# Queries and keys through a bf16 copy in DRAM and DMA transposes, from the fourth batch on

## The chip, the cores and the metric

The kernel runs on one core of one Trainium2 chip. The metric is the time of one execution on the device in microseconds; the time before is the median of three runs. The engines are PE (TensorE, matmuls), DVE (VectorE), ACT (ScalarE), POOL (GpSimd) and SP (SyncE, which here only issues DMAs).

## The reference

Sparse attention over 8 batches of 8 heads, 576 positions of 64 numbers, followed by a bilinear feed-forward layer over the 4608 tokens. The first four heads of a batch attend to a local window, the other four to positions with the same residue modulo 32.

```python
scores = scale * np.matmul(q, k.transpose(0, 1, 3, 2))          # q, k, v: (8, 8, 576, 64)
rel = pos[:, None] - pos[None, :]
mask_local = (rel >= 0) & (rel < 32)
mask_strided = (rel >= 0) & (pos[None, :] % 32 == pos[:, None] % 32)
masks = [mask_local if h < 4 else mask_strided for h in range(8)]
attn = softmax(np.where(masks, scores, -1e9))
x = np.matmul(attn, v).transpose(0, 2, 1, 3).reshape(4608, 512)
out = ((x @ w_a) * (x @ w_b)) @ w_out                            # w_a, w_b: (512, 1536)
```

## The kernel before

**Tiles and slots.** The feed-forward layer is cut into nine tiles of 512 tokens (t = 0 to 8), and each tile into 16 slots: twelve `ffn_ab` (the two products of one block of 128 hidden columns, multiplied by DVE into `pf`) and four for the output product. Slot 16t+i is the i-th slot of tile t. A matmul result of `ffn_ab` sits in one of four PSUM banks (`mm` three, `tp` one): ACT copies the first product out (`a_sb`), DVE's `pf` multiply (line 648 or 650) frees the second. The output product of tiles 2 to 8 works with sums of blocks of `pf` (`ps`, made by DVE in `fast_s`, line 760), and tiles 7 and 8 do the same for the first products (`joint`), which needs sums of the weights `wa_sb` and `wb_sb`: `wsum_make` (line 666) makes eight of 128x1536, each in two instructions, the four of `wa_sb` on DVE and the four of `wb_sb` on POOL, in tile 6.

**Attention runs between the slots.** The attention of batch b is put into tile b-1; tile b is the first to need its result. It has eight units u: S (`S_p`, scores of two heads, line 389), exp on ACT, the mask on DVE (line 428), then V (`step_VT`, line 527, or `V_p`, line 467). `LATER` is the plan from batch 3 on, in slots of that tile: S0 at -1, V0 at 1, and so on to V5 at 11; `IN_Y` puts the rest into the output product. There is one `o` PSUM buffer, so the next V waits until DVE has taken the last one's result (lines 541 and 543 for batch 2 and the strided heads, after ACT's Ln and Exp at lines 536 and 537; line 493 for the local heads). Local results of batches 3 to 7 go to DRAM (`rows_out`, `xd`, step O) and come back transposed into `xT` (`rows_in`, step I, line 514, a DMA transpose on SP).

**How q and k come in, from batch 2 on.** POOL issues DMAs that cast to bf16, a head at a time: `load_qk`, line 213 for local heads into `kl` and `ql`, line 204 for strided heads into `natk` and `natq`. DVE transposes blocks of 32x32 (`step_D`, lines 328 and 333) into `tk` and `tq`. SP then moves them with DMAs from SBUF to SBUF (lines 343 and 347) into `kT` and, with zeros between, into `qz` (the zeros let one matmul with 128 rows serve two heads). `kT` and `qz` have two buffers, for odd and even batches. In the code, g0 = 16(b-2) is the first slot of tile b-2, in which batch b is brought in.

**Order.** Nothing is reordered: every engine, SP and POOL included, works through its own instructions in the order in which the program gives them. `do(i, ...)` puts a step behind slot i. From slot 14 on, POOL's part of a slot waits for that slot's `pf` or `y_sb` (a copy into `pace`, line 1060), so that its DMAs go out slot by slot. SP has no such pace: it goes on until a semaphore holds it.

Of the kernel before, what the change touches and what calls it, by code (L numbers as in the profile page):

```python
# [8 lines left out]
BF16 = mybir.dt.bfloat16  # L9
I16 = mybir.dt.int16  # L10
ALU = mybir.AluOpType
# [3 lines left out]
FIRST_D = 2  # L15
RL = 6
RS = 8
# [14 lines left out]
def kernel(  # L32
# [228 lines left out]

    held = {}
    paired = {}

# [54 lines left out]
    def step_D(b, z, nm, part):  # L321
        src = nats[b, nm, z == 1]
        if part == 0:
            tl[b, z, nm] = blocks(nm, z)
        t = tl[b, z, nm]
        if z == 0:
            i = slice(NY // 2 * part, NY // 2 * (part + 1))
            nc.vector.transpose(t.rearrange("p h (i y) -> p i h y", i=NY)[:, i],
                                src[:, i].rearrange("p i (h d) -> p i h d", h=2))
            last = part == 1  # L330
        else:

            nc.vector.transpose(
                t.rearrange("p h (r c) -> p r h c", r=RS)[:, :, :, YS * part:YS * part + 32],
                src[:, part].rearrange("p (r h d) -> p r h d", r=RS, h=2))
            last = part == 2
        if last:
            for nm, c in {"k": (("k", 0),), "q": (("q", 0), ("k", 1), ("q", 1))}[nm]:
                t = tl[b, z, nm]
                for e in range(2):  # L340
                    if nm == "k":
                        dst = kT_buf[b % 2][z][64 * e:64 * e + 64, c]
                        nc.sync.dma_start(out=dst[:, PAD:] if z == 0 else dst[:, :RS * GP], in_=t[64 * c:64 * c + 64, e])
                        continue
                    for j in range(2):
                        r0 = 64 * c + 32 * j
                        nc.sync.dma_start(out=qz_buf[b % 2][j][z][64 * e + 32 * j:64 * e + 32 * j + 32, c],
                                          in_=t[r0:r0 + 32, e])
                if (nm, c, z) == ("q", 0, 0) and b - 1 > FIRST_D:
                    rows_in(b - 1, 1)  # L350

    def rezero(b):

        for j in range(2):
            for t in qz_buf[b % 2][j]:
                nc.gpsimd.memset(t[32:64] if j == 0 else t[64:96], 0.0)

    def step_Tk(b, c):
        T_p(b, c, "k")
# [19 lines left out]
    def S_p(b, u):  # L379
# [4 lines left out]
        held[b, "st", u] = st  # L384
        if b > 0:
            sv = st.rearrange("p a (i n) -> p (a i) n", n=256)
            for i in range(G):
                k0 = (G * half + i) * (LW if c < 2 else GP)
                nc.tensor.matmul(sv[:, i, :2 * n].rearrange("p (j n) -> p j n", j=2), lhsT=kT[:, c % 2, k0:k0 + 128],  # L389
                                 rhs=qz_pair[b % 2][c // 2][:, :, c % 2, k0:k0 + n], start=True, stop=True)  # L390
            return
# [124 lines left out]
    def step_VT(b, u):  # L516
# [4 lines left out]
        for i in range(G):  # L521
            for j in range(2):
                if c < 2:
                    vt = vl_buf[b % 2][:, (2 * c + j) * 6 + 3 * half + i]
                else:
                    vt = vs_buf[b % 2][:, 2 * (c - 2) + j, 4 * half + i]
                nc.tensor.matmul(o[:, j, i * n:(i + 1) * n], lhsT=vt, rhs=p_cols(b, p, j, i, n, n)[:M], start=True, stop=True)  # L527

        r = sb.tile([128, RS * 4 * D], BF16, tag="xr", name="xr", bufs=2)[:64, :4 * W].bitcast(F32)
        r = r.rearrange("p (j w) -> p j w", j=2)  # L530
        if c < 2:
            sums = o[64:, :, :W]
# [33 lines left out]
    def step_X(b, c):  # L566
# [20 lines left out]
    LATER = {-1: "S0", 0: "S1", 1: "V0", 2: "S2", 3: "V1 O0", 4: "S3", 5: "V2", 6: "S4 I0", 7: "V3 O1", 8: "S5", 9: "V4",  # L587
             10: "S6",
             11: "V5"}
    IN_Y = {2: "S7", 6: "V6", 11: "V7"}  # L590
# [36 lines left out]
    def ffn_ab(t, f, mid, ab=None):  # L627
# [28 lines left out]
    wsum = [[h.rearrange("p (c g m) -> p c g m", c=2, g=FG) for h in homes] for homes in (  # L656
        [flat(vl_buf[0])[:, WS * z:WS * (z + 1)] for z in range(2)] + [flat(t)[:, :WS] for t in qz_pair[0]],
        [flat(vs_all[0])[:, WS * z:WS * (z + 1)] for z in range(2)] + [flat(nat_s[nm]) for nm in "qk"])]
    xsum = {t: flat(qz_pair[1][t - 7])[:, :8 * HT].rearrange("p (n c m) -> p n c m", n=4, c=2) for t in JOINT}

    def wsum_make(s, n, eng):
        w, s_ = (lambda e, j: wviews[s][:, j, :, :, e]), wsum[s]
        a, b, op = ((w(1, 0), w(1, 1), ALU.add), (s_[0], w(0, 0), ALU.subtract), (w(0, 0), w(1, 0), ALU.subtract),
                    (w(0, 1), s_[1], ALU.subtract))[n]
        for c in range(2):
            eng.tensor_tensor(s_[n][:, c], a[:, c], b[:, c], op=op)

    def x_part(t, j, k):
        x0 = TTOK * t % (XR * S) + HT * k
# [30 lines left out]
    def joint(t):  # L700
# [3 lines left out]
        for half, (plain, *gs) in enumerate(JOINT[t]):  # L704
            banks = {x: eight(x) for x in "Ya Yb Xb Zb Xa Za".split()}
            order = JOINT_ORDER[half].split()
            for at_, (k, m) in enumerate(order):
# [10 lines left out]
                else:  # L718
# [4 lines left out]
                    bank = banks[bank + m]  # L723
                    for s in range(2):
                        for c in range(2):
                            w = wsum[s][lhs][:, c, g] if isinstance(lhs, int) else wviews[s][:, lhs[1], c, g, lhs[0]]
# [182 lines left out]
    with tc.manual_schedule(engines={ENG.PE, ENG.SP, ENG.Pool, ENG.DVE, ENG.Activation}):  # L909
# [77 lines left out]
        for b in range(1, B):  # L987
            for pos, names in (STEPS.get(b) or {16 * (b - 1) + x: n for x, n in LATER.items()}).items():
                steps.setdefault(pos, []).append((b, names.split()))
            if b not in STEPS:  # L990
                for n, names in IN_Y.items():
                    steps["y", b - 1, n] = [(b, names.split())]
        steps[16 * (B - 2) + 9][-1][1].append("I1")

        at = {}

# [12 lines left out]
        for b in range(FIRST_D, B):  # L1009
            g0 = 16 * (b - 2)  # L1010
            if b == FIRST_D:
# [82 lines left out]
```

## Time and profile before

| | |
|---|---|
| Runs | 330.39, 330.40, 331.71 us, median 330.4 |
| Profiled execution | 331.63 us, span 329.9 us |
| TensorE clock | 1.0 throughout |
| Busy, share of the span | PE 96%, DVE 81%, PEld 64%, ACT 57%, POOL 55% |
| DMA queue of POOL | 85968 packets, 19.48 MB, 64.7% of 16 engines' span |
| DMA queue of SP | 25772 packets, 20.71 MB, 26.0% |
| Tile 1 from | 58 us (slot 16) |
| Tiles 2, 3, 4, 5, 6 from | 94, 128, 161, 195, 229 us |

The span is the profiled stretch; the execution's own time has 1.7 us around it. A line of a timeline reads: start, duration, engine, line, operation, output<-input, shape, count, and in brackets how long the engine was idle before it and who released it. A line of the waits reads: who waited for whom, total, number of waits, longest.

### The profile page before, as it was taken

To read this page: it belongs to the slowest core of one execution; us is meant where nothing else is said; L and a number is where in the kernel's file an instruction comes from. 1 tells how busy PE (TensorE), PEld (TensorE's weight loads), DVE (VectorE), ACT (ScalarE), POOL (GpSimd) and SP (SyncE) were. 2 spreads that over 40 slices of the span, in tenths; PEclk is the share of its full clock that TensorE was granted. 3 is DMA by queue.
4 is the path that set the end of the run, shared out by engine and by line. 5 is a ranking of instruction groups with operands and counts; after the bars stand their busy time and mean duration, and the time that the engine had idled before them with its cause. 6 is when DMAs were issued, how large, how long until landed. Compare 5 with 4: busy or idle time off the path is not lost.

```text
span 329.9 us, 7496 instructions
## 1 busy us (share of the span) xinstructions
PE 317.1 (96%) x2691; PEld 212.8 (64%) x2720; DVE 267.3 (81%) x551; ACT 188.7 (57%) x320; POOL 180.2 (55%) x295
## 2 busy tenths in 40 slices
PE   8999999999999999999999999999986799999995
PEld 6754555445555586557999875578543577787775
DVE  7766887888778889889889888988999977864882
ACT  6764764468764575457644764476544555525532
POOL 8845836899857444754475347632278405312350
PEclk9999999999999999999999999999999999999999
DMA  9999999899999999999999999998164013003003
GB/s 158 149 204 201 203 182 168 185 182 130 141 211 130 135 100 92 124 208 121 119 120 215 123 114 107 188 171 103 31 173 59 0 24 108 0 0 129 2 1 127
DMA packets 111920, 40.73 MB, mean 123 GB/s; under 512 B 89868, under 2 KB 108940, under 8 KB 111884
## 3 DMA queue, kind: packets, MB, share of 16 engines
q0 software_dynamic: 85968, 19.48, 64.7%
q1 hardware_dynamic: 25772, 20.71, 26.0%
q8 instruction: 21, 0.34, 0.4%
q14 instruction: 15, 0.12, 0.1%
q10 hardware_dynamic: 144, 0.07, 0.1%
HBM read 39.51 MB, written 11.06 MB: 153 GB/s over the span
## 4 chain that ended last, share of the span: by engine, by line
PE 72%; DMA 8%; DVE 8%; POOL 7%; issue 3%; ACT 1%; POOLq 0%; DVEq 0%
PE mm L624 32%; PE mm L818 13%; PE mm L880 5%; DMA vl<-in_v_dram 4%; DMA shared<-in_q_dram 4%; PE st L389 3%; PE o L527 2%; PE eA L624 2%; PE eXb L728 2%; PE eXa L728 2%; PE eB L624 2%; DVE ps L760 2%; POOL shared L198 2%; PE eYa L818 2%; DVE pf L648 2%
## 5 line engine op out<-in xcount | busy, mean ns | idle before, releaser
L624 PE MATMUL mm<-xT,wb_sb 128*128 128x512 bf16 (+1 forms) x373 | 85.0, 352 | 4.2 <-DVE pf L648 3.9
L624 PE MATMUL mm<-xT,wa_sb 128*128 128x512 bf16 (+1 forms) x360 | 83.9, 351 | 0.7
L645 ACT COPY a_sb<-mm 128x512 f32<-128x512 f32 x82 | 47.9, 585 | 49.0 <-PE mm L624 41.5
L624 PEld LDWEIGHTS <-wb_sb 128*128 128x128 bf16 x416 | 40.1, 98 | 39.9 <-issue 5.2
L624 PEld LDWEIGHTS <-wa_sb 128*128 128x128 bf16 x416 | 37.3, 98 | 22.7 <-DVE xT L543 0.3
L1060 POOL CAST pace<-pf 1x1 f32<-1x1 bf16 x71 | 22.8, 321 | 45.2 <-DVE pf L648 31.8
L648 DVE TENSOR_TENSOR pf<-a_sb,mm 128x512 bf16<-128x512 f32 x60 | 40.7, 679 | 6.4 <-PE mm L624 6.1
L410 ACT ACTIVATE p<-st 72x576 bf16<-72x576 f32 (+1 forms) x56 | 36.4, 650 | 16.2 <-PE st L389 16.0
L543 DVE TENSOR_TENSOR xT<-o,xr 64x288 bf16<-64x288 f32 x48 | 21.4, 445 | 13.5 <-ACT xr L537 13.0
L818 PEld LDWEIGHTS <-ps 128*128 128x128 bf16 x288 | 27.9, 98 | 3.9 <-DVE ps L760 0.7
L732 POOL TENSOR_TENSOR pf<-vl 128x256 bf16<-128x256 f32 x12 | 8.7, 729 | 30.8 <-DVE vl L741 30.8
L536 ACT ACTIVATE xr<-o 64x576 f32<-64x576 f32 x28 | 18.1, 647 | 12.6 <-PE o L527 12.3
L880 PE MATMUL mm<-wo_sb,pf 128*128 128x512 bf16 x93 | 23.2, 379 | 0.2
L818 PEld LDWEIGHTS <-pf 128*128 128x128 bf16 x216 | 20.1, 98 | 3.7 <-DVE pf L648 1.2
L244 POOL DMA_DIRECT2D vs<-in_v_dram x24 | 19.6, 818 | 5.0 <-PE mm L818 2.4
L760 DVE TENSOR_TENSOR ps<-pf 128x512 bf16<-128x512 bf16 (+2 forms) x42 | 21.6, 514 | 0.6
L818 PE MATMUL mm<-wf,ps 128*128 128x256 bf16 x180 | 21.5, 273 | 0.5 <-DVE ps L760 0.5
L537 ACT ACTIVATE xr<-xr 64x576 f32<-64x576 f32 x28 | 19.1, 683 | 0.9
L213 POOL DMA_DIRECT2D ql<-in_q_dram x24 | 15.9, 664 | 6.2 <-DMA wo_sb<-in_moe_w_out_dram 4.6
L213 POOL DMA_DIRECT2D kl<-in_k_dram x24 | 16.1, 671 | 5.3 <-issue 3.2
L791 ACT COPY y_sb<-mm 128x512 f32<-128x512 f32 x20 | 11.7, 585 | 12.1 <-PE mm L818 10.5
L650 DVE TENSOR_TENSOR pf<-a_sb,mm 128x512 bf16<-128x512 f32 x22 | 14.9, 677 | 4.5 <-ACT a_sb L645 2.7
(242 smaller groups left out, 640.0 us busy)
## 6 DMA issues: line engine op xcount, KB each, us to landing
out_dram<-y_sb SPq DMA_DIRECT2D x12, 512.0 KB, 5.5
out_dram<-y_sb SPq DMA_DIRECT2D x11, 256.0 KB, 4.2
vl<-in_v_dram POOLq DMA_DIRECT2D x6, 384.0 KB, 7.7
kl<-in_k_dram POOLq DMA_DIRECT2D x24, 72.0 KB, 3.1
ql<-in_q_dram POOLq DMA_DIRECT2D x24, 72.0 KB, 3.3
vs<-in_v_dram POOLq DMA_DIRECT2D x24, 72.0 KB, 4.2
wo_sb<-in_moe_w_out_dram POOLq DMA_DIRECT2D x4, 384.0 KB, 9.8
natk<-in_k_dram POOLq DMA_DIRECT2D x20, 72.0 KB, 3.5
```

Source lines behind the costliest of these rows:

```text
L213: nc.gpsimd.dma_start(out=t[32 * h:32 * h + 32], in_=src[b, h].rearrange("(i y) d -> y i d", y=32))
L244: nc.gpsimd.dma_start(out=vs_buf[b % 2][:, h, :, 0:D], in_=v[b, HL + h].rearrange("(p r) d -> p r d", r=RS))
L410: nc.scalar.activation(p_flat(p)[:M, :2 * W].rearrange("p (i n) -> p i n", n=2 * n), st[:M].rearrange("p a (i n) -> p (a i) n", n=256)[:, ...
L537: nc.scalar.activation(r, r, ACT.Exp, scale=-1.0)
L543: nc.vector.tensor_mul(dst.rearrange("d (p r) -> d p r", r=RS)[:, :, G * half:G * (half + 1)], o[:64, j, :W].rearrange("d (g p) -> d p g", ...
L624: nc.tensor.matmul(ps_[:, c0:c0 + n], lhsT=w[:, kk, 128 * f:128 * (f + 1)], rhs=xT[:, kk, x0:x0 + n], start=(kk == first and c0 == 0), sto ...
L645: nc.scalar.copy(a_sb, ab[0])
L648: nc.vector.tensor_mul(pf[:, f, :].rearrange("p (i a s) -> p a i s", i=2, s=16), halves(a_sb), halves(ab[1]))
L760: nc.vector.tensor_tensor(s[:, n], a, b, op=op)
L818: nc.tensor.matmul(bank[b][:, q], lhsT=lhs(g, q), rhs=rhs(g), start=k in "172" and q == 0 and g == 0, stop=g == FG - 1, skip_group_check=True)
L880: nc.tensor.matmul(ybank[j], lhsT=pf[:, f, 128 * j:128 * (j + 1)], rhs=wo_sb[:, f], start=(f == 0), stop=(f == FD - 1))
L1060: nc.gpsimd.tensor_copy(pace, done)
```

## The change

For batches 3 to 7, q and k go another way. POOL casts the local and the strided heads of k and of q into DRAM, four DMAs per batch in place of sixteen (`rows_load`, slots g0+1 to g0+4). SP brings each in by one DMA transpose (`rows_take`, slots g0+4, 6, 8, 10), keys straight into `kT`, queries into `tq`. DVE copies the queries' halves into the padded `qz` (`rows_pad`, slots g0+8, 9 for the local heads, g0+12, 13 for the strided ones). DVE's block transposes and SP's 24 transfers from SBUF to SBUF remain for batch 2 only.

With it: the strided heads are in another order, so `S_p` and `step_VT` take one head a unit, in as many matmuls of the same sizes, and `step_VT` writes 64x576 in one multiply. `rezero` clears other halves of the other `qz` buffer and moves from slot 14 to slot 33. `rows_in(b, 1)` moves to slot 9 of its tile for all batches. All sixteen weight-sum instructions are DVE's, eight in tiles 4 and 5 and eight in tile 6, at other places in SBUF.

```diff
+    def rows_load(b, nm, z):
+        t = rows[nm, z] = dram.tile([(S, NR)[z], (4, 8)[z] * D], BF16, tag=f"z{nm}{z}", name=f"z{nm}{z}", bufs=1)
+        h0 = b * H + HL * z
+        src = {"k": k, "q": q}[nm].rearrange("b h s d -> (b h) s d")[h0:h0 + HL]
+        if z:
+            nc.gpsimd.dma_start(out=t.rearrange("(h p) m -> h p m", h=HL), in_=src.rearrange("h (p r) d -> h p (r d)", r=RS))
+        else:
+            nc.gpsimd.dma_start(out=t.rearrange("s (h d) -> s h d", d=D), in_=src.rearrange("h s d -> s h d"))
+
+    def flat_s(t):
+        return t.rearrange("p c n -> p (c n)")[:, :4 * NR]
+
+    def rows_take(b, nm, z):
+        t = kT_buf[b % 2][z] if nm == "k" else blocks("q", z)
+        if nm == "q":
+            tl[b, z, nm] = t
+        dst = flat_s(t).rearrange("p (i m) -> p i m", i=4) if z else t[:, :, PAD:] if nm == "k" else t
+        nc.sync.dma_start_transpose(out=dst, in_=rows.pop((nm, z)))
+
+    def rows_pad(b, z, j):
+        dst, src = (flat_s(t)[64 * j:64 * j + 64] for t in (qz_pair[b % 2][z][:, j], tl[b, z, "q"]))
+        nc.vector.tensor_copy(dst, src)
+
+    def rezero(b):
+        for z in range(2):
+            for j in range(2):
+                nc.gpsimd.memset(qz_pair[b % 2][z][64 - 64 * j:128 - 64 * j, j], 0.0)
...
-                if (nm, c, z) == ("q", 0, 0) and b - 1 > FIRST_D:
-                    rows_in(b - 1, 1)
...
+            if b > FIRST_D and c >= 2:
+                kf = kT.rearrange("p c n -> p (c n)")
+                for i in range(G):
+                    k0 = i * NR + (u - HL) * NP
+                    nc.tensor.matmul(sv[:, i, :2 * n].rearrange("p (j n) -> p j n", j=2), lhsT=kf[:, k0:k0 + 128],
+                                     rhs=qz_pair[b % 2][1].rearrange("p j c n -> p j (c n)")[:, :, k0:k0 + n],
+                                     start=True, stop=True)
+                return
...
+        if b > FIRST_D and c >= 2:
+            by_token = lambda x: x[:, :, :W].rearrange("d j (g p) -> d p g j", p=NP)
+            r = r.rearrange("d (p g j) -> d p g j", g=G, j=2)
+            nc.scalar.activation(r, by_token(o[64:]), ACT.Ln)
+            nc.scalar.activation(r, r, ACT.Exp, scale=-1.0)
+            dst = xT[64 * half:64 * half + 64, c, S * (b % XR):S * (b % XR + 1)]
+            nc.vector.tensor_mul(dst.rearrange("d (p g j) -> d p g j", g=G, j=2), by_token(o[:64]), r)
+            return
...
-    LATER = {-1: "S0", 0: "S1", 1: "V0", 2: "S2", 3: "V1 O0", 4: "S3", 5: "V2", 6: "S4 I0", 7: "V3 O1", 8: "S5", 9: "V4",
+    LATER = {-1: "S0", 0: "S1", 1: "V0", 2: "S2", 3: "V1 O0", 4: "S3", 5: "V2", 6: "S4 I0", 7: "V3 O1", 8: "S5", 9: "V4 I1",
...
-        for c in range(2):
-            eng.tensor_tensor(s_[n][:, c], a[:, c], b[:, c], op=op)
+        nc.vector.tensor_tensor(made(n), a, b, op=op)
...
-        steps[16 * (B - 2) + 9][-1][1].append("I1")
...
+                for n, (z, nm) in enumerate(((0, "k"), (0, "q"), (1, "k"), (1, "q"))):
+                    do(g0 + n + 1, rows_load, b, nm, z)
+                    do(g0 + 2 * n + 4, rows_take, b, nm, z)
+                    if nm == "q":
+                        for j in range(2):
+                            do(g0 + 2 * n + 6 + j, rows_pad, b, z, j)
                 for h in range(HL):
-                    do(g0 + h + (2 if b == FIRST_D + 1 else -2), load_qk, b, False, (h,))
-                    do(g0 + h + (6 if b == FIRST_D + 1 else 2), load_qk, b, True, (h,))
                     do(g0 + h + 10, load_vs, b, (h,))
                 do(g0 + (10 if b == FIRST_D + 1 else 7), load_vl, b)
-            gs = {2: (14, 14, 15, 15, 16, 16, 17, 17, 18, 18), 3: (8, 9, 10, 11, 12, 13, 14, 15, 16, 17)}.get(b) or (
-                3, 5, 7, 9, 12, 13, 14, 15, 16, 17)
+                continue
+            gs = (14, 14, 15, 15, 16, 16, 17, 17, 18, 18)
...
-        for n in range(4):
-            do(16 * (NT - 3) + 2 * n + 2, wsum_make, 0, n, nc.vector)
-            do(16 * (NT - 3) + 2 * n + 3, wsum_make, 1, n, nc.gpsimd)
+        for n in range(16):
+            do(16 * (NT - 5) + 3 * n + 1 if n < 8 else 16 * (NT - 3) + 2 * (n - 8), wsum_make, n // 8, n // 2 % 4, n % 2)
...
-        do(14, rezero, 1)
         do(28, fill_v, vs_buf[1])
+        do(33, rezero, 0)
```

More of the change, by code (lines that the diff above doesn't have):

```diff
@@ L259, in load_wo @@
         )
+    rows = {}
+    NR = HL * S // RS
+    def rows_load(b, nm, z):
[21 more added lines that the diff above has]
+                nc.gpsimd.memset(qz_pair[b % 2][z][64 - 64 * j:128 - 64 * j, j], 0.0)
     held = {}
@@ L348, in step_D @@
                                           in_=t[r0:r0 + 32, e])
-                if (nm, c, z) == ("q", 0, 0) and b - 1 > FIRST_D:
-                    rows_in(b - 1, 1)
[L352 to L356, printed above, removed]
     def step_Tk(b, c):
@@ L524, in step_VT @@
                     vt = vl_buf[b % 2][:, (2 * c + j) * 6 + 3 * half + i]
+                elif b > FIRST_D:
+                    vt = vs_buf[b % 2][:, u - HL, 2 * i + j]
                 else:
@@ L655, with wsum_home, wsum_make @@
     WS = 2 * FG * 128
-    wsum = [[h.rearrange("p (c g m) -> p c g m", c=2, g=FG) for h in homes] for homes in (
-        [flat(vl_buf[0])[:, WS * z:WS * (z + 1)] for z in range(2)] + [flat(t)[:, :WS] for t in qz_pair[0]],
-        [flat(vs_all[0])[:, WS * z:WS * (z + 1)] for z in range(2)] + [flat(nat_s[nm]) for nm in "qk"])]
-    xsum = {t: flat(qz_pair[1][t - 7])[:, :8 * HT].rearrange("p (n c m) -> p n c m", n=4, c=2) for t in JOINT}
[L661 to L664, printed above, removed]
-        for c in range(2):
-            eng.tensor_tensor(s_[n][:, c], a[:, c], b[:, c], op=op)
+    wsum = {}
+    def wsum_home(i):
+        if i < 2:
+            at_ = ([nat.tile([128, NY, D], BF16, tag=f"{nm}l", name=f"{nm}l") for nm in "kq"] if i == 0 else
+                   [blocks("k", z) for z in range(2)])
+            at_ = [flat(t)[:, :WS // 2] for t in at_]
+        else:
+            at_ = (flat(nat_s["kq"[i - 2]]) if i < 4 else flat(vl_buf[0])[:, WS * (i - 4):WS * (i - 3)] if i < 6 else
+                   flat(qz_pair[0][i - 6])[:, :WS])
+            at_ = [at_[:, WS // 2 * c:WS // 2 * (c + 1)] for c in range(2)]
+        return [t.rearrange("p (g m) -> p g m", g=FG) for t in at_]
+    xsum = {t: flat(qz_pair[1][t - 7])[:, :8 * HT].rearrange("p (n c m) -> p n c m", n=4, c=2) for t in JOINT}
+    def wsum_make(s, n, c):
+        if c == 0:
+            wsum[s, n] = wsum_home(4 * s + n)
+        w, made = (lambda e, j: wviews[s][:, j, c, :, e]), (lambda n: wsum[s, n][c])
+        a, b, op = ((lambda: (w(1, 0), w(1, 1), ALU.add)), (lambda: (made(0), w(0, 0), ALU.subtract)),
+                    (lambda: (w(0, 0), w(1, 0), ALU.subtract)), (lambda: (w(0, 1), made(1), ALU.subtract)))[n]()
+        nc.vector.tensor_tensor(made(n), a, b, op=op)
     def x_part(t, j, k):
@@ L725, in joint @@
                         for c in range(2):
-                            w = wsum[s][lhs][:, c, g] if isinstance(lhs, int) else wviews[s][:, lhs[1], c, g, lhs[0]]
+                            w = wsum[s, lhs][c][:, g] if isinstance(lhs, int) else wviews[s][:, lhs[1], c, g, lhs[0]]
                             x = xsum[t][:, rhs, c] if isinstance(rhs, int) else x_part(t, *rhs)[:, c]
```

## The prediction

> **What bounds the kernel now.** I read the page first, then the busy time by stage, then the waits of PE, then the timelines of DVE, POOL, SP and PE around the places found.
>
> ```profile
> PE 317.1 (96%) x2691; PEld 212.8 (64%) x2720; DVE 267.3 (81%) x551; ACT 188.7 (57%) x320; POOL 180.2 (55%) x295
> ```
>
> PE is idle for 12.8 us of 329.9, so removing work from DVE, POOL, SP or the DMA engines can give at most part of that. The stages show where the idle time lies (length, PE busy, PEld, DVE, ACT, POOL, clock, DMA, GB/s):
>
> ```profile
> 222.00:224.00 2.00, 2.00 (x26) 1.82 (x24) 1.96 (x5) 1.21 (x3) 1.77 (x4) 1.00 0.67 64
> 244.00:246.00 2.00, 1.61 (x12) 0.76 (x12) 2.00 (x3) 0.38 (x1) 2.00 (x2) 1.00 0.99 262
> 248.00:250.00 2.00, 0.92 (x6) 0.31 (x4) 1.97 (x6) 0.70 (x2) 1.31 (x3) 1.00 0.90 63
> 254.00:256.00 2.00, 0.92 (x5) 0.34 (x4) 2.00 (x6) 0.67 (x2) 1.33 (x1) 1.00 0.34 73
> ```
>
> From 96 to 244 us PE is full almost everywhere. In 244 to 263 us (tile 6) it is not, and DVE is at 100%. The waits of PE name DVE, and in the timeline all six lie there:
>
> ```profile
> PE mm L624 <- DVE pf L648: 3.9, 4, 1.1
> PE mm L818 <- DVE pf L648: 0.9, 1, 0.9
> PE mm L818 <- DVE ps L760: 0.5, 1, 0.5
> ```
>
> They are 0.88, 1.08, 0.81, 1.08, 0.94 and 0.47 us, together 5.3 us. The timelines of DVE and POOL tell why:
>
> ```profile
> 239.73 1.93 DVE L428 TENSOR_TENSOR p<-p,mask_l 128x576 int16<-128x576 int16 x1 [0.17 <-ACT p L410]
> 244.14 1.75 DVE L760 TENSOR_TENSOR ps<-pf 128x512 bf16<-128x512 bf16 x1
> 245.82 0.67 DVE L648 TENSOR_TENSOR pf<-a_sb,mm 128x512 bf16<-128x512 f32 x1
> ...
> 238.11 3.23 POOL L666 TENSOR_TENSOR vs<-wb_sb 128x768 bf16<-128x768 bf16 x2
> 243.80 3.72 POOL L666 TENSOR_TENSOR vs<-vs,wb_sb 128x768 bf16<-128x768 bf16 x2
> ```
>
> While POOL makes its eight weight sums, DVE's SBUF-to-SBUF operations take 1.15 to 1.93 us in place of 0.41 to 0.46; the `pf` multiply, which reads PSUM, keeps 0.67. Over the seven stretched operations the excess is 1.47+1.34+0.98+1.35+0.99+0.91+0.74 = 7.8 us.
>
> **What the change gives.** POOL's eight sums are gone; DVE makes all sixteen. In tile 6 DVE still makes eight (0.55 us each, as before), the other eight come in tiles 4 and 5. So DVE loses 7.8 us of stretching there and gets nothing for it: more than the 5.3 us that PE waited. I take the whole **-5.3 us**, low end -4.3 if one wait stays.
>
> The rest that goes is cover, not path. DVE, batches 3 to 7: 20 transposes of 0.766 and 30 of 0.704 go (36 us); 20 pad copies come. Their price has no row: a 72x512 copy is 0.378, a 128x1280 memset 0.59; bounds 0.4 to 0.8, I take 0.7 as 1152 elements are nearest the latter (14 us). One 64x576 multiply replaces two of 64x288 (2 x 0.445, about 0.75 if the length alone is doubled), 20 times: 3 us less. POOL: 80 issues of about 0.64 go, 20 come: the local ones with 2304 packets lie between kl's 0.66 (576 packets) and vl's 1.46 (3072), taken 1.25; the strided ones with 16 large pieces 0.6. SP: 120 issues of about 0.6 go, 20 transposes come. PE and ACT keep their count and sizes. None of this ended a wait of PE in tiles 1 to 5, so its value there is nothing; if a cover fails it is in the waits that come.
>
> **The waits that come.** Each `rows_pad` stands in DVE's order and waits for a DMA transpose; behind it stand the `pf` multiplies that free PE's banks and the xT multiplies that free the one `o` bank. The transposes stand in SP's order behind the casts that POOL issues, slot by slot. So I date each landing against the moment when DVE gets there. The nearest row for a transpose is half as large (576 pieces of 256 B; now 1152):
>
> ```profile
> L514 SPq DMA_TRANSPOSE xT<-xd x11: 1128/1211/2598, 49.3 to 252.7; - x11
> DMA to landing us min/median/max: 2.6/4.5/7.4
> ...
> 72.28 2.50 SPq L347 DMA_DIRECT2D qz0s<-tq  x4
> 146.68 2.60 SPq L514 DMA_TRANSPOSE xT<-xd  x1
> ...
> 78.28 0.91 DVE L541 TENSOR_TENSOR xT<-o,xr 64x288 bf16<-64x288 f32 x2 [0.26 <-ACT xr L537]
> ...
> 79.52 0.42 PE L527 MATMUL o<-p,vl 128*128 128x96 bf16 x6
> ```
>
> Plain issues take 0.5 to 0.6 whatever their size, the transpose 1.13. Issue of the double size: 1.13 (no growth) to 2.26; I take 2.1, growth over a 0.5 base with a little less. In the undisturbed one (252.67) the packets ran for 0.9 us after the issue had ended and it landed 2.6 after its start. The double: 2.1 + 1.8 + 0.6 = 4.5 from its start, at worst 7.4, as the one at 146.68 that ran beside the v load of its slot.
>
> Batch 3 (tile 1). SP is busy with batch 2's 24 transfers until 74.8 and comes to k's transpose only then; q's starts at 76.9 and lands at 81.4. DVE gets to the first pad (slot 24) at 77.2, in place of the transpose at 77.23, and sits there until 81.4, copies until 82.1, then does the xT pair (0.91) that the V step at 79.52 needs: it starts at 83.3 (with its old gap of 0.3). **+3.8 us**; 0.7 with an issue of 1.13, a landing of 2.6 and the cheap copy, 6.8 with a landing of 7.4.
>
> Batch 4 (tile 2). `rezero`, moved from slot 14 to 33, puts POOL's four memsets (1.05, 1.16, 1.05, 1.16: 4.4 us) between the casts of k and q. Slot 33's pace ends at 98.9: k's cast is issued at 99.2, q's at 105.4. A cast's landing: kl's 576 packets 2.6 at least, vl's 3072 7.1 (window 100 to 130); less the issues, (5.64-1.94)/156 = 24 ns per packet and engine, 1.1 fixed. 2304 packets: 1.25+1.1+3.5 = 5.8. So q's cast lands at 111, its transpose starts there, beside the v load of 110.9, and lands at 115.5 to 118.4, taken 117; pad done 117.7. By batch 5's limit, a tile (33.7 us) earlier, PE loses from 115.3 on: **+2.4 us**; nothing with a landing of 2.6, 3.9 with 7.4.
>
> Batches 5 to 7. In tile 3: k's cast 132.9 to 138.7, q's behind it to 142.2. SP: k's transpose 138.7 to 140.8, then xT's I0, which waits for `xd` (issued 136.9, landing 4.8) to 141.7, then q's from 142.9, landing 147.4 to 150.3. DVE gets to the pad at about 146.2. Behind it: ps 0.38, pf 0.67, xT 0.75; the V step at 150.80 needs that, so a pad done by 149.0 is free. Done at 148.1 to 151.0: 0 to 2.0, taken 1.0 each, **+3.0 us** for three. The strided pads (slots 60, 61): I1 now stands at slot 57, ahead of the last transpose, which goes out at 151.0, lands at 155.5 against a pad due at 155.2, and the xT behind it waited for ACT until 157.49: nothing; 1.9 each if it lands in 7.4 (copy and ps end at 159.8, 2.3 behind 157.49, of which 0.4 is slack before the V step at 158.78). Output stores stand behind the transposes on SP, but DVE and ACT need their buffers a tile later: nothing.
>
> Sum: -5.3 + 3.8 + 2.4 + 3.0 = **+3.9 us**. The profiled execution took 331.63 (span 329.9 and 1.7 around it): 335.5. It stands 1.23 above the median of 330.4, to which I add the same: **334.3 us**.
>
> [...]
>
> **Rivals.** (1) Pads in time: the big transposes issue in 1.13 and land in 2.6 like the small one, casts as dated. Then batch 3 costs 0.7 and the others nothing: -4.6, **325.8 us**. For it: the lone transpose at 2.6, and DMA queues freed of 120 small transfers. Against it: SP's 74.8 in tile 1 and the memsets ahead of q's cast in tile 2. It decides once q's transpose lands before 79 us in tile 1 and 115 in tile 2.
> [...]
> (3) DVE stays short in tile 6 in spite of POOL's silence: no gain, +9.2, **339.6 us**. Against it stands `ps` at 0.41 in the tiles without POOL's sums.
> (4) Gain and waits cancel: batch 3 at 2, batch 4 at 1.5, the rest at 0.6 each: **330.4 us**.
>
> **Numbers.** My forecast has 0.45, (1) 0.25, (2) 0.08, (3) 0.07, (4) 0.15. A measurement here can tell about 0.5% (1.7 us) from no change. Faster 0.25 is (1); same 0.15 is (4); slower 0.60 is the forecast with (2) and (3). Range: the low ends of all terms are rival (1)'s 325.8; the high ends are -4.3+6.8+3.9+6.0+5.7 = +18.1, 348.5, which takes every landing at its worst. I begin at 325.5 and stop at 345, and so leave out (2) and a sliver on each side. The forecast's own range is 332.1 (1.7 above the median; below that it is case 4) to 338.0 (each wait half way to its high end: 5.3+3.1+4.5-5.3 = +7.6).
>
> **What would show it.** Right: no wait of PE on DVE pf in tile 6 and masks at 0.45 there; waits of DVE on `qz1l<-tq` by DMA of 3 to 5 us in tile 1 and about 4 in tile 2, with PE idle behind each. Wrong: pads without a wait before them, casts landing far from 6 us, big transposes issued in 1.2, or DVE still full in tile 6.

## The result and the profile after

The changed kernel takes 364.3 us (median of 362.74, 364.15, 364.53 and 368.67) against 330.4 before; the ratio is 1.100, interval 1.0952 to 1.1048. The ratios, but not the medians, leave out runs that lie more than 1.5% above the fastest of their kernel: 368.67 here, and one each in experiments 1 (852.35), 3 (347.73, two slots later), 4 (351.18), 5 (362.58) and 10 (370.62). I had said 334.3 with a range to 345. The profiled execution took 362.74 (span 361.0): 31 us more than the profiled one of before.

The page's first part, busy time by engine, and the waits of DVE's copies and of PE:

```profile
PE 326.1 (90%) x2691; PEld 217.7 (60%) x2720; DVE 240.6 (67%) x509; ACT 188.7 (52%) x320; POOL 126.0 (35%) x214
```

```profile
DVE qz1l L288 <- DMA tq<-zq: 22.7, 3, 8.3
PE mm L665 <- DVE pf L689: 21.6, 4, 6.1
DVE qz0l L288 <- DMA tq<-zq: 15.0, 2, 7.6
PE o L560 <- DVE xT L582: 5.9, 1, 5.9
```

DVE has 27 us and POOL 54 us less to do, as the change says. But DVE now sits idle for 37.7 us ahead of the first local pad copy (line 288), once in each of the batches 3 to 7, until the transpose of q (`tq<-zq`) has landed; behind it PE is idle five times, 27.6 us in all. PE waits for DVE nowhere else, but for 0.2 us at 51 us and 0.3 us in the last tile, which the kernel before has too. DVE's timeline has the five waits, 7.1 to 8.3 us each:

```profile
83.81 0.45 DVE L288 COPY qz1l<-tq 64x1152 bf16<-64x1152 bf16 x1 [7.10 <-DMA tq<-zq]
128.24 0.45 DVE L288 COPY qz0l<-tq 64x1152 bf16<-64x1152 bf16 x1 [7.44 <-DMA tq<-zq]
169.42 0.45 DVE L288 COPY qz1l<-tq 64x1152 bf16<-64x1152 bf16 x1 [7.27 <-DMA tq<-zq]
210.97 0.45 DVE L288 COPY qz0l<-tq 64x1152 bf16<-64x1152 bf16 x1 [7.56 <-DMA tq<-zq]
252.79 0.45 DVE L288 COPY qz1l<-tq 64x1152 bf16<-64x1152 bf16 x1 [8.30 <-DMA tq<-zq]
```

Batch 5, from the timelines of POOL and SP: the casts, an output store, the transposes and the v load that lead to the third of them.

```profile
148.60 1.65 POOL L274 DMA_DIRECT2D zk<-in_k_dram  x1 [0.33 <-issue]
150.75 1.62 POOL L274 DMA_DIRECT2D zq<-in_q_dram  x1 [0.47 <-issue]
152.45 0.51 POOL L272 DMA_DIRECT2D zk<-in_k_dram  x1
153.37 0.61 SPq L865 DMA_DIRECT2D out_dram<-y_sb  x1
154.28 4.80 SPq L284 DMA_TRANSPOSE kT1l<-zk  x1
154.35 0.51 POOL L272 DMA_DIRECT2D zq<-in_q_dram  x1 [0.29 <-issue]
159.14 2.20 SPq L545 DMA_TRANSPOSE xT<-xd  x1
160.30 1.46 POOL L226 DMA_DIRECT2D vl<-in_v_dram  x1 [0.38 <-PE mm L665]
161.43 1.69 SPq L284 DMA_TRANSPOSE tq<-zq  x1
```

k's transpose takes 4.80 us to issue, where the one at 112.95 in batch 4, which landed 3.5 us after its start, took 1.28; xT's behind it takes 2.20; q's goes out at 161.43, beside the v load, and lands 8.0 later. DVE had been ready since 162.15 (169.42 less 7.27). The output store of 512 KB goes out on SP just ahead of k's transpose in batches 5, 6 and 7 (153.37, 194.10 and 235.28); in batch 4 none stands there. The DMA engines are busy all that time (columns: length; PE; PEld; DVE; ACT; POOL; clock; DMA share; GB/s; the share is the time that the packets took over that of 16 engines, and here it passes 1):

```profile
152.00:156.00 4.00, 4.00 (x27) 2.03 (x26) 2.94 (x7) 1.82 (x3) 1.74 (x6) 1.00 1.76 125
156.00:160.00 4.00, 3.95 (x27) 2.08 (x27) 3.26 (x8) 1.91 (x4) 0.38 (x3) 1.00 1.34 239
160.00:164.00 4.00, 4.00 (x30) 2.10 (x29) 1.78 (x4) 2.68 (x5) 1.89 (x2) 1.00 1.17 196
164.00:168.00 4.00, 1.81 (x12) 0.84 (x10) 0.00 (x0) 1.60 (x3) 0.00 (x0) 1.00 1.71 147
```

Tile 6, the place of the expected gain, did become what was forecast. Its stages (same columns) and DVE's timeline there:

```profile
276.00:278.00 2.00, 2.00 (x13) 1.03 (x11) 1.29 (x3) 1.26 (x3) 0.17 (x1) 1.00 0.41 83
284.00:286.00 2.00, 2.00 (x14) 1.03 (x12) 1.69 (x5) 1.25 (x3) 0.17 (x1) 1.00 0.41 82
```

```profile
277.66 0.46 DVE L459 TENSOR_TENSOR p<-p,mask_l 128x576 int16<-128x576 int16 x1 [0.17 <-ACT p L441]
278.04 0.55 DVE L718 TENSOR_TENSOR vl<-vl,wb_sb 128x768 bf16<-128x768 bf16 x1
278.51 0.41 DVE L812 TENSOR_TENSOR ps<-pf 128x512 bf16<-128x512 bf16 x1
```

PE is full, masks are back at 0.46 and `ps` at 0.41, with the weight sums of 0.55 between them.

The granted clock was 1.0 throughout before. Now it has gaps, 6.8 us at half speed behind each wait. PE's timeline and the stages around batch 4's wait (same columns):

```profile
123.44 1.03 PE L665 MATMUL mm<-xT,wa_sb 128*128 128x512 bf16 x4
129.67 1.86 PE L665 MATMUL mm<-xT,wb_sb 128*128 128x512 bf16 x4 [5.21 <-DVE pf L689]
```

```profile
126.00:128.00 2.00, 0.00 (x0) 0.00 (x0) 0.00 (x0) 0.00 (x0) 0.00 (x0) 0.91 2.08 196
128.00:130.00 2.00, 0.33 (x1) 0.10 (x1) 1.76 (x4) 0.29 (x1) 0.17 (x1) 0.50 0.70 132
130.00:132.00 2.00, 2.00 (x13) 1.07 (x12) 1.92 (x5) 0.29 (x1) 0.06 (x1) 0.50 0.70 131
132.00:134.00 2.00, 2.00 (x12) 1.38 (x10) 1.97 (x5) 1.33 (x2) 1.45 (x3) 0.50 0.42 90
```

Four matmuls of 512 columns take 1.86 us in place of 1.03, and in the same 6 us DVE is full too (1.76 to 1.97 of 2.00): it works off what it could not do while it waited. Which of the two sets the pace there is asked in the last experiment, which does not settle it.

### The profile page after: what moved, and what is told of

Read it like the earlier page. It is cut to its first block, busy times and chain, and to the rows that moved or that the text cites. A ratio compares the mean times of both kernels' runs of the same rounds, so it can differ in the third digit from the quotient of the medians.

```text
span 361.0 us, 7100 instructions
## 1 busy us (share of the span) xinstructions
PE 326.1 (90%) x2691; PEld 217.7 (60%) x2720; DVE 240.6 (67%) x509; ACT 188.7 (52%) x320; POOL 126.0 (35%) x214
## 4 chain that ended last, share of the span: by engine, by line
PE 65%; DMA 20%; POOL 7%; DVE 3%; SPq 2%; issue 2%; DVEq 0%; POOLq 0%
PE mm L665 27%; PE mm L870 14%; DMA tq<-zq 11%; PE mm L932 4%; DMA wb_sb<-in_moe_w_b_dram 4%; DMA vl<-in_v_dram 4%; PE o L560 2%; SPq L545 2%; PE st L420 2%; PE eA L665 2%; PE eXa L780 2%; PE eXb L780 2%; DMA zq<-in_q_dram 2%; PE eB L665 2%; POOL shared L198 2%
## 5 line engine op out<-in xcount | busy, mean ns | idle before, releaser
L665 PE MATMUL mm<-xT,wb_sb 128*128 128x512 bf16 (+1 forms) x373 | 89.2, 365 | 21.9 <-DVE pf L689 21.6
L665 PEld LDWEIGHTS <-wb_sb 128*128 128x128 bf16 x416 | 41.0, 100 | 59.2 <-issue 25.0
L1114 POOL CAST pace<-pf 1x1 f32<-1x1 bf16 x67 | 16.3, 244 | 147.1 <-DVE pf L689 84.7
L870 PEld LDWEIGHTS <-pf 128*128 128x128 bf16 x216 | 22.0, 107 | 4.0 <-POOL pf L784 0.2
L569 DVE TENSOR_TENSOR xT<-o,xr 64x576 bf16<-64x576 f32 x20 | 15.0, 749 | 13.1 <-ACT xr L567 12.9
L932 PE MATMUL mm<-wo_sb,pf 128*128 128x512 bf16 x93 | 23.3, 383 | 0.2
L870 PE MATMUL mm<-wf,ps 128*128 128x256 bf16 x180 | 21.3, 273 | 0.0
L870 PE MATMUL mm<-wo_sb,pf 128*128 128x256 bf16 x120 | 19.3, 316 | 0.0
L812 DVE TENSOR_TENSOR ps<-pf 128x512 bf16<-128x512 bf16 (+2 forms) x42 | 18.9, 449 | 0.6
L566 ACT ACTIVATE xr<-o 64x576 f32<-64x576 f32 x20 | 12.9, 647 | 12.1 <-PE o L560 11.9
L691 DVE TENSOR_TENSOR pf<-a_sb,mm 128x512 bf16<-128x512 f32 x22 | 14.9, 678 | 4.8 <-ACT a_sb L686 2.6
L288 DVE COPY qz1l<-tq 64x1152 bf16<-64x1152 bf16 x6 | 2.7, 455 | 22.7 <-DMA tq<-zq 22.7
L459 DVE TENSOR_TENSOR p<-p,mask_l 128x576 int16<-128x576 int16 x32 | 14.5, 453 | 3.7 <-ACT p L441 3.6
```

The lines of the kernel that those rows point to most:

```text
L459: nc.vector.tensor_tensor(pi, pi, mk, op=ALU.bitwise_and)
L569: nc.vector.tensor_mul(dst.rearrange("d (p g j) -> d p g j", g=G, j=2), by_token(o[:64]), r)
L665: nc.tensor.matmul(ps_[:, c0:c0 + n], lhsT=w[:, kk, 128 * f:128 * (f + 1)], rhs=xT[:, kk, x0:x0 + n], start=(kk == first and c0 == 0), sto ...
L691: nc.vector.tensor_mul(pf[:, f, :], a_sb, ab[1])
L812: nc.vector.tensor_tensor(s[:, n], a, b, op=op)
L870: nc.tensor.matmul(bank[b][:, q], lhsT=lhs(g, q), rhs=rhs(g), start=k in "172" and q == 0 and g == 0, stop=g == FG - 1, skip_group_check=True)
```

## The experiments

Twelve kernels in three groups; each is compared with runs of the kernel before that were made with its group (medians 331.02, 330.77 and 331.02 us). The theory: the whole loss is DVE's wait for q's local transpose, because the pads stand at a slot that the transpose cannot meet; it is late through what stands ahead of it on POOL and SP and what shares the DMA engines with it. The rivals: the casts' small writes to DRAM are dear; one single neighbour (memsets, large strided pieces, v load) is the culprit; PE's half clock is a loss of its own.

**1. The sums alone.** The kernel before, with POOL's half of the weight sums on DVE:

```diff
-            do(16 * (NT - 3) + 2 * n + 3, wsum_make, 1, n, nc.gpsimd)
+            do(16 * (NT - 3) + 2 * n + 3, wsum_make, 1, n, nc.vector)
```

> One part of the change alone: the kernel before, with POOL's eight weight sums of tile 6 moved to DVE, at the slots where POOL had them; queries and keys come in as before. If POOL's sums were what stretched DVE (7.8 us) and so made PE wait (5.3 us), DVE now gets 8 x 0.55 = 4.4 us of sums and loses the 7.8: 325 to 327 us, no wait of PE on pf in tile 6, masks at 0.45 there. Rival: DVE is short in tile 6 anyway, so that 4.4 us more of work keep PE waiting: 330 to 333 us.

Measured: 326.41 us, ratio 0.986 (0.9844 to 0.9876): 4.6 us less. That part of the change is a gain by itself, and close to the 5.3 that I had put down. In tile 6 PE still waits for `pf` twice, 0.32 and 0.99 us, where I had expected no wait.

**2. Only the pads later.** The changed kernel, with the copies of the local heads four slots later and those of the strided heads five:

```diff
-                            do(g0 + 2 * n + 6 + j, rows_pad, b, z, j)
+                            do(g0 + (12 if z == 0 else 17) + j, rows_pad, b, z, j)
```

> The changed kernel, with only the pad copies later: local ones behind slots g0+12 and 13 in place of 8 and 9, strided ones behind g0+17 and 18 in place of 12 and 13. If the five waits of DVE on a transpose (37.7 us in the trace) with PE's idle time and the half clock behind them are the whole loss, they vanish: 330.4 - 5.3 = 325, 324 to 328 us, clock 1.0. Rival: the casts and transposes are too slow as traffic, and the wait moves to S0, to the strided pads or to the stores: 335 us or more.

Measured: 324.72 us, ratio 0.9812 (0.9797 to 0.9827), faster than both kernels. The page:

```profile
PE 315.5 (98%) x2691; PEld 213.0 (66%) x2720; DVE 240.8 (75%) x509; ACT 188.8 (58%) x320; POOL 127.6 (40%) x214
```

PE waits for DVE only the 0.3 us in the last tile, and DVE waits for q twice, 1.9 us in all. The transposes did not get faster: q's take a median of 7.2 us from issue to landing here, 5.2 in the changed kernel. The local ones land 19.6 to 22.4 us after the issue of k's cast (19.2 to 21.8 in the changed kernel), and DVE now comes to them at 21.3 to 21.8: these slots just meet the landings. So the 39.6 us between the two kernels are the place of the copies, not the price of casts or transposes.

**3. One slot and two slots later.** Between those two:

```diff
-                            do(g0 + 2 * n + 6 + j, rows_pad, b, z, j)
+                            do(g0 + 2 * n + 7 + j, rows_pad, b, z, j)
```

and the same with `+ 8`.

> The changed kernel, with every pad copy one slot (about 2 us) later. If a wait costs what it is long, five waits shorter by 2 us give 364 - 10 = 354 us. [...]

> Every pad two slots later than in the changed kernel (one slot later gave 354.3 us and waits of 3.8, 3.8, 5.0, 5.6 and 5.5 us). If the landings stay where they are, each wait falls by a slot's 1.9 us or more, PE is idle for 0 to 1 us in batches 3 and 4 and for about 3 in 5 to 7, where half the clock loss stays: 334 to 342 us. If the landings come later with the pads, as one slot suggested in batches 5 to 7, the waits there stay at 4.5 or more and the time at 345 to 350.

Measured: 354.26 us (ratio 1.0686, 1.0653 to 1.0719) and 338.0 us (1.018, 1.0116 to 1.0244). The first slot gave 10 us, the second 16. One slot later the waits are 3.76, 3.80, 5.02, 5.62 and 5.46, two slots later 2.15, 3.34, 3.33, 3.76 and 3.25. In batches 5 to 7 they shrink by 1.9 to 2.8 us with the first slot and by 1.7 to 2.2 with the second, about the length of a slot: the landings stay where they are. The half clock did not go with the shorter waits. PE's idle times one slot later were 2.47, 2.90, 4.67, 5.22 and 4.57 us, and behind the two shortest there were still 3.4 and 6.8 us of half clock. Two slots later it came at two waits of about 1 us each in batches 5 and 7, and did not come at two equal ones in batch 4, nor at 1.91 and 1.12 us in batch 6.

**4. v out of the way.** The changed kernel with `load_vl` at slot g0+13:

```diff
-                do(g0 + (10 if b == FIRST_D + 1 else 7), load_vl, b)
-                continue
+                do(g0 + 13, load_vl, b)
+                continue
```

> The changed kernel, with only the load of v's local heads (3072 small packets) moved from slot g0+7 (g0+10 for batch 3) to g0+13, behind the first pads. If that load beside it is why the queries' transpose takes 7 to 9 us to land (3.5 where nothing ran beside it), batches 4 to 7 land about 4 us earlier, DVE waits 3 to 4 us and PE under 2 each, without the half clock: 364 - 4 x 7 = about 336 us. Rival: the delay lies ahead of it (casts, SP's issues that take 4 to 5 us): waits stay over 5.5 us, 355 us or more. Batch 3 should stay as it is in both, since its v load comes later anyway.

Measured: 348.58 us (1.0504, 1.0452 to 1.0556): the direction, but little more than half of the gain that was expected. The waits of batches 4 to 6 fall to 3.95, 3.67 and 2.89; those of batches 3 and 7 stay, at 6.97 and 7.77. Batch 3 has SP's backlog: in the changed kernel SP comes to k's transpose only at 75.57, behind batch 2's transfers. In batch 7, k's transpose (issued in 5.31), xT's (2.89) and q's (2.81) were slow without any v load; why more so than in batches 5 and 6, I did not find out. The v load costs 3.5 to 4.7 us of wait in batches 4 to 6, but it is not the cause alone.

**5. The memsets.** `rezero` out from between batch 4's casts:

```diff
-        do(33, rezero, 0)
+        do(31, rezero, 0)
```

> Asks what batch 4's wait of 7.44 us comes from. If it is POOL's four memsets standing between the casts of k and q (4.4 us), the cast of q goes out 4.4 us earlier, its transpose gets ahead of the v load of that tile, the wait falls to 3 us or less and the time by 5 to 8 us: 356 to 359 us; the other four waits stay at 7.1 to 8.3. If it is what also makes batches 5 to 7 wait (they have no memsets), the wait stays at 6 to 7 us and the time at 363 to 364.

Measured: 358.75 us (1.079, 1.0768 to 1.0811), 5.6 less. Batch 4's wait fell from 7.44 to 4.17, less than expected, for k's transpose in front now met the casts' traffic and issued in 3.01 in place of 1.28. DVE's timeline, batches 4 and 5:

```profile
124.35 0.45 DVE L288 COPY qz0l<-tq 64x1152 bf16<-64x1152 bf16 x1 [4.17 <-DMA tq<-zq]
165.11 0.45 DVE L288 COPY qz1l<-tq 64x1152 bf16<-64x1152 bf16 x1 [8.60 <-DMA tq<-zq]
```

The memsets are 3.3 us of batch 4's wait and nothing of the others'.

**6. The strided casts: smaller pieces, and later.** First the same bytes in 288 pieces of 1 KB in place of 16 of 18 KB (36 KB as read, in f32), by longer rows in DRAM:

```diff
-        t = rows[nm, z] = dram.tile([(S, NR)[z], (4, 8)[z] * D], ...)
+        t = rows[nm, z] = dram.tile([(S, NR)[z], (4, 9)[z] * D], ...)
...
-            nc.gpsimd.dma_start(out=t.rearrange("(h p) m -> h p m", h=HL), ...)
+            nc.gpsimd.dma_start(out=t[:, :8 * D].rearrange("(h p) m -> h p m", h=HL), ...)
...
-        nc.sync.dma_start_transpose(out=dst, in_=rows.pop((nm, z)))
+        nc.sync.dma_start_transpose(out=dst, in_=rows.pop((nm, z))[:, :(4, 8)[z] * D])
```

then the same casts two slots later (`do(g0 + n + 1 + 2 * z, rows_load, b, nm, z)`, their pads at slots 17 and 18).

> Asks whether the strided casts' 16 pieces of 36 KB are what stretches the issue of k's transpose to 4.8 to 5.5 us in batches 5 to 7 (1.3 where it runs alone) and so delays q's behind it. Here the rows of the strided DRAM tiles are 64 elements longer than what is used, so the same bytes go in 288 pieces of 1 KB. If the large pieces are the cause, k's transpose issues in 1.3 to 2 us, q's starts some 3.5 us earlier, the waits of batches 5 to 7 fall to 3 to 5 us and the time to 350 to 356. If any traffic of that size does it, the issue stays at 4 to 5 and the time at 362 to 366.

> Asks whether it is the strided casts at all that slow k's local transpose: they are issued two slots later (their pads at slots 17 and 18 of the batch, where they cost nothing), so in batches 5 to 7 they begin some 4 us behind k's transpose in place of beside it. If they are the cause, by their pieces or their bytes, k's transpose issues in under 3 us, the waits of batches 5 to 7 fall to 3 to 5 us and the time to 350 to 356. If it is the local cast of q (2304 small packets), which is in flight at the same time, the issue stays at 4 to 5 us and the time at 360 to 365.

Measured: 362.61 us (1.0952, 1.0921 to 1.0983) and 363.35 us (1.0995, 1.0934 to 1.1056): neither can be told from the changed kernel. With small pieces k's transpose issued in 3.7 to 3.9 in batches 5 to 7, but q's, behind it, in 3.5 in place of 1.5 to 1.7. With the casts later it was 2.7 to 3.6 for k's, and the strided casts now ran beside q's. Both shifted the crowd from one transpose to the next. One neighbour was not moved in any run, the output store just ahead of k's transpose in batches 5 to 7. In batch 4, without it, that transpose issued in 1.28 us, and in 3.01 with the casts beside it (experiment 5). How much of the 4.8 to 5.5 us is the store's stays open.

**7. q before k.** The two local casts and transposes change places:

```diff
-                for n, (z, nm) in enumerate(((0, "k"), (0, "q"), (1, "k"), (1, "q"))):
+                for n, (z, nm) in enumerate(((0, "q"), (0, "k"), (1, "k"), (1, "q"))):
```

> q's local cast and transpose change places with k's (pads at the same slots as in the changed kernel). If the wait is made by what stands ahead of q's transpose (k's transpose in SP's order, the memsets in POOL's), q's transpose starts where k's did, 5 to 7 us earlier; even with a landing of 9 us it is in by the pad's slot or 2 us behind it: waits of 0 to 2 us in each batch, PE loses little and the clock stays, 326 to 334 us. If the late landing is made by what runs beside it (v load, casts), the waits stay at 4 us or more in batches 4 to 7 and the time is 345 or more.

Measured: 358.33 us (1.0836, 1.0787 to 1.0885). The local waits did fall, to 3.95, 1.29 and 2.26 in batches 5 to 7 and none in batch 4 (batch 3 kept 6.37). But the strided pads, which had waited for nothing in the changed kernel, now wait in their place. DVE's timeline, batches 6 and 7:

```profile
201.04 0.45 DVE L288 COPY qz0l<-tq 64x1152 bf16<-64x1152 bf16 x1 [1.29 <-DMA tq<-zq]
215.00 0.45 DVE L288 COPY qz0s<-tq 64x1152 bf16<-64x1152 bf16 x1 [5.97 <-DMA tq<-zq]
242.68 0.45 DVE L288 COPY qz1l<-tq 64x1152 bf16<-64x1152 bf16 x1 [2.26 <-DMA tq<-zq]
257.02 0.45 DVE L288 COPY qz1s<-tq 64x1152 bf16<-64x1152 bf16 x1 [6.82 <-DMA tq<-zq]
```

They too stand at a slot that their transposes do not meet; the local wait ahead of them had only given the DMAs the time. DVE's waits sum to 37.7 us here as well.

**8. All three moved.** q first, v late, strided pads at 17 and 18, local pads at their early slots:

> Three of the things that stood beside or ahead of q's local transpose are moved at once: q's cast and transpose before k's, the v load of the tile six slots later, the strided pads to slots 17 and 18; the local pads stay at their early slots. If order and company on the saturated DMA queues are the whole cause, batches 4 to 7 wait 0 to 1.5 us and only batch 3, where SP is busy with batch 2's transfers until 75, keeps its 6 us: 331 to 336 us. If the early slot cannot be met whatever the order, waits of 3 us or more stay in batches 5 to 7 and the time is over 345.

Measured: 332.96 us (1.0064, 1.0039 to 1.0088), as the theory had it. Batch 3 keeps 5.47, batches 4 to 7 wait 0 to 1.66 each:

```profile
DVE qz1l L288 <- DMA tq<-zq: 8.0, 3, 5.5
...
DVE qz0l L288 <- DMA tq<-zq: 1.7, 1, 1.7
```

DVE's waits are 28.0 us less than with q before k alone. Of these, 23.8 are the strided pads' waits, which end because those copies stand later, as in experiment 2; only 4.2 are the local pads'. The company is not gone: in batches 5 to 7 the first transpose behind the casts issues as slowly as before and lands 9.1 to 9.4 us after its start. SP's timeline, batch 5:

```profile
145.90 4.88 SPq L284 DMA_TRANSPOSE tq<-zq  x1
150.84 2.26 SPq L545 DMA_TRANSPOSE xT<-xd  x1
153.21 1.31 SPq L284 DMA_TRANSPOSE kT1l<-zk  x1
```

q's transpose comes nearly in time because it starts 7 to 8 us earlier. So in batches 5 to 7 its place behind two slow transposes on SP is the larger part of the lateness. The v load is another part (experiment 4), and the memsets are one in batch 4 (experiment 5). How the three changes of this kernel share the 25 us from 358.33, it does not separate.

**9. The sums inside the changed kernel.** The kernel with late pads, with eight sums back on POOL:

```diff
-        nc.vector.tensor_tensor(made(n), a, b, op=op)
+        (nc.gpsimd if s else nc.vector).tensor_tensor(made(n), a, b, op=op)
```

> The kernel with late pads (local at slots 12 and 13, strided at 17 and 18; 324.7 us), with eight of the sixteen weight sums back on POOL at their new slots. Prices the sums by themselves inside the changed kernel. If DVE is stretched beside POOL as in the kernel before, the sums in tile 6 give back 2 to 5 us: 327 to 330 us, with DVE's SBUF operations at 1.1 us or more there. If the stretch only cost time because DVE was full with other work, which is gone now, 324 to 326.

Measured: 326.43 us (0.9863, 0.9839 to 0.9887), 1.7 more than with all on DVE: between the two ranges. The stretch is there (a mask of 2.03, a `ps` of 1.68), but DVE has no sums of its own in that tile now and room for most of it; one wait of PE of 1.4 us is left. With POOL making its half of the sums this kernel is still 4.6 us faster than the kernel before, as much as the sums alone gave in experiment 1, and both together give 6.3. So the two gains overlap: each relieves DVE in tile 6.

**10. The half clock.** The changed kernel with 64 matmuls that nobody reads, ahead of the matmul that waits in batches 4 to 7:

```diff
+    def fill(i):
+        if i in (43, 59, 75, 91):
+            out = last_st[0].rearrange("p a (i n) -> p (a i) n", n=256)[:, :2, 192:]
+            for _ in range(64):
+                nc.tensor.matmul(out, lhsT=wa_sb[:, 0, :128], rhs=wb_sb[:, 0, :128].rearrange("p (i n) -> p i n", i=2), start=True, stop=True)
...
-            mid = lambda: take(i - 0.5)
+            mid = lambda: (take(i - 0.5), fill(i))
```

> The changed kernel with 64 matmuls of 128 columns that nobody reads, written to unused columns of a PSUM bank ahead of the matmul that waits in batches 4 to 7 (some 4 us of PE's work in each 5 to 6 us of waiting; batch 3 has none). The waits on q's transposes stay. If PE's half clock comes from its own idle time, the clock stays full in those four places and the 2 to 2.5 us that each loses at half clock are saved: 354 to 357 us although PE does more work. If the clock falls for another reason, or costs nothing, 363 to 366.

Measured: 362.74 us (1.0878, 1.082 to 1.0936), just under the second range. The clock stayed full in one of the four places only, batch 6; in batches 4, 5 and 7 it still fell, for 3.4 us in place of 6.8. In all it is at half speed for 17 us in place of 34. But these stretches now lie behind PE's wait and not partly in it, so the time that PE works at half clock falls only from 21.1 to 14.9 us: 3.1 us to be gained by PE's count, half of the difference. The time fell by 1.6 us in the medians and by about 4 in the ratios. The profiled execution was 1.4 us longer, with DVE's waits 3.0 us longer (40.7 for 37.7). The waits:

```profile
DVE qz1l L288 <- DMA tq<-zq: 24.6, 3, 8.8
DVE qz0l L288 <- DMA tq<-zq: 16.1, 2, 8.6
...
PE mm L878 <- DVE pf L697: 1.8, 2, 0.9
```

The new wait in the last line, 0.9 us each in batches 5 and 6, is DVE's backlog: PE reaches `pf` banks that DVE has not freed yet. From the pad copy of batches 4, 5 and 6 to the next batch's first cast it is 20.36, 20.30 and 19.97 us in the changed kernel, 19.72, 20.82 and 19.12 with the fill: 0.6 less, 0.5 more and 0.9 less, where PE's count gives 0.7, 0.6 and 2.0 less. So the run does not decide the question. The 8 to 10 us that I expected were not there to be gained, as the clock fell in spite of the fill; whether the half clock is a loss of its own stays open.

**What the waits cost.** The profiled executions side by side, against the kernel with late pads (span 322.9, waits 1.9):

| kernel | DVE's waits for q, us, over late pads | span over late pads, us |
|---|---|---|
| changed | 35.7 | 38.1 |
| memsets earlier | 34.5 | 35.4 |
| small strided pieces | 33.0 | 37.8 |
| strided casts later | 34.4 | 39.0 |
| q before k | 35.7 | 34.2 |
| fill | 38.7 | 39.5 |
| v late | 23.3 | 21.2 |
| pads one slot later | 21.7 | 29.8 |
| pads two slots later | 13.9 | 14.6 |
| q first, v late, strided pads late | 7.7 | 8.2 |

But for one row, each microsecond that DVE waits costs 0.9 to 1.15 us of the whole (third column by second). With pads one slot later it is 1.4. PE's own time accounts for both kinds of row, as idle time behind DVE and, as an estimate from the four matmuls that took 1.86 us in place of 1.03, half of the time that it works at half clock: 27.6 and 10.6 us of the 38.1 in the changed kernel, 19.8 and 9.2 of the 29.8 with pads one slot later. So more of DVE's wait reaches PE there; why, no run shows.

Taken by batch, from one first cast to the next and against the same distance with late pads, the clock does seem to count. Waits of 3.3 to 4.2 us cost 1.5 to 3.7 us in five places where the clock stayed full (two slots later, batches 4 and 6; v late, batches 4 and 5; memsets earlier, batch 4), and 3.8 and 5.1 us in two where it fell (two slots later, batch 5; one slot later, batch 4). Seven places in different kernels, one execution each, do not prove it.

## Why the prediction was wrong

**Right: the direction, the mechanism and its five places.** DVE waits before the first local pad in batches 3 to 7 and PE behind it, in the two forms that I had named (the V step's `o` bank in batch 3, `pf` banks in the others).

**Right: tile 6.** -5.3 was put down; the sums alone give 4.6 in the kernel before. Rival (3), DVE still short there, falls by the shown timeline. What I had called worth nothing, DVE's relief from the transposes, is worth something in that tile too: by experiment 9 the change gives 4.6 us even with POOL's sums in place.

**Right: the small prices.** The local casts land in 5.4 to 6.0 us (k) and 6.0 to 8.0 (q), estimated 5.8. The copies take 0.455 for 0.7, the 64x576 multiply 0.749 for 0.75. That small writes to DRAM are dear, the case of rival (2), no run shows: the strided casts, with pieces of 18 KB, land no sooner (6.1 to 9.6 us) than the local ones with 128 B.

**Right in place, short in size: batch 3.** q's transpose starts at 77.34, forecast 76.9, and DVE was ready at 76.71, forecast 77.2. It landed 6.4 us after its start, not 4.5: 7.1 us of DVE's wait against 4.2, and 5.94 us of PE's idle time against 3.8. The same holds for batch 4: the memsets are 3.3 us of its wait by experiment 5, but q's transpose landed 8.5 us after its start, for 4.5 to 7.4, and PE was idle for 5.21 against 2.4.

**Wrong: the terms of batches 5 to 7, 1.0 each of PE's time; PE was idle for 5.05, 5.29 and 6.07 us in DVE's waits of 7.3 to 8.3.** By the prediction's own steps, counted in batch 5 from the issue of k's cast: k's transpose starts at +5.7 (forecast +5.8) and DVE is ready at +13.55 (forecast +13.3). Between them three terms were too small. The issue of k's transpose took 4.80 in place of 2.1, and 5.54 and 5.08 in batches 6 and 7. With xT's transpose behind it, 2.20, q's started at +12.8 in place of +10.0. It landed 8.0 after its start, for 4.5 to 7.4. That is +20.8 for +14.5 to +17.4.

The step that failed is the price of the big transposes beside other traffic. I took the issue from the undisturbed row (1.13, doubled to 2.1), kept the disturbed landing of 7.4 us as the worst case and went by the middle. Measured in batches 5 to 7 are 4.8 to 5.5 us of issue for k's, beyond all that I had allowed, and 7.2 to 8.8 of landing for q's: the worst case is the ordinary one. What runs alone does not double at all, 1.28 us of issue and 3.5 of landing for twice the pieces. The disturbed row that I had shown, 2.60 us of issue beside a v load, gives 5.2 when doubled; as the company is another one, that this comes near may be chance. I had also read plain issues as "0.5 to 0.6 whatever their size". SP's timeline of before has pairs, issued behind an output store, that took 2.5 and 4 times their usual 1.18 us:

```profile
143.27 2.96 SPq L343 DMA_DIRECT2D kT1l<-tk  x2
211.10 4.74 SPq L343 DMA_DIRECT2D kT1l<-tk  x2
```

And I had put the output stores behind the transposes, where one stands just ahead of k's. With this went the high end of the sum: "every landing at its worst" was 348.5.

**Wrong: the slack, and nothing behind it.** I counted 2.8 us between the pad's slot and the V step that needs its successors as free. It is, at that place: PE goes on for 3.7 us after DVE has stopped in batch 4 (120.80 to 124.46) and idles 5.21 in a wait of 7.44. But from cast to cast that wait costs 6.8 us. PE's idle times are 27.6 us together, where the sum had 9.2, and PE then works 10.6 us longer than with late pads (326.1 for 315.5), at half clock, for which the sum had no term. In the same stretches DVE works off its backlog; which of the two takes these 10.6 us stays open.

**Held only by luck: the strided pads at nothing.** They wait for nothing in the changed kernel because the local pads' wait moved DVE past their landings, by 2.3 to 2.7 us in batches 4 to 7. Where q comes before k and the local waits are smaller, they wait 5.5 to 6.8 us (experiment 7). I had set aside a case of 1.9 us each, for a landing in 7.4. With a local wait of 1 us as forecast, these rows give more, by an estimate 3.8 us in batch 5 (the wait of 7.3, less 1.0, less 2.5 by which the landing was early).

**Rival (1)**, pads in time, 325.8: the kernel with late pads measured 324.7. The sum without waits came within about 1 us, in part by luck, since the gain is not the sums' alone (experiment 9). The rival's own reason does not hold: in that kernel q's transposes land in 4.5 to 9.6 us and not in 2.6.

## What to carry to other kernels

Where a DMA's landing is due in an engine's program order, price it from a row that runs in the same company, not from the undisturbed one. If the DMA engines are busy throughout the stretch (shares of 1.17 to 1.76 here), take the disturbed value as the ordinary case. Waits of 7 to 8 us on an engine that feeds the bottleneck were paid almost in full here, though the bottleneck had cover for 3.7 us at that moment. Place the consumer where the worst landing is in: that cost nothing here and turned a loss of 34 us into a gain of 6. When one wait is removed, look at the next instruction that depends on the same queue, for it may have been covered by the first.

## What was not expected of the hardware

The issue of a DMA transpose on SP is itself stretched by traffic: 1.28 us in batch 4 ahead of the traffic, 4.8 to 5.5 beside casts and an output store, and everything behind it on SP waits as long. Moving the v load away did not change that for the first transpose behind the casts (4.76 to 5.31 us in batches 5 to 7).

The granted clock falls to 0.50 behind PE's idle times of 5.05 to 6.07 us for 6.8 us. That it also fell behind idle times of 2.5 and 2.9 us (one slot later, for 3.4 and 6.8 us), and at two waits of about 1 us each (two slots later), was not expected. PE worked in only 21.1 of the 34.1 us at half clock, and its busy time is 10.6 us longer than with late pads.
